# Second group's partial outputs through ScalarE and an adding DMA, lead copies on ScalarE, and passes taken group by group

## The chip, the cores and the metric

The program runs on one core of a Trainium2 chip. The metric is device time in microseconds (us) for one execution. Names of engines are those of the profile: PE (TensorE), with PEld for its weight loads, DVE (VectorE), ACT (ScalarE), POOL (GpSimd) and SP (SyncE, which here only issues DMAs). DMAs can be issued from SP, ACT and POOL; each of these works through its own list of instructions in order, and an instruction that waits holds everything behind it on the same engine.

## The reference

Local attention with a few global tokens, then a two-layer network with an ELU between the layers (sizes: batch 8, 8 heads, 512 local and 32 global tokens, head width 64; network 512 to 2048 to 512).

```python
def _attn_ref(q_l, k_l, v_l, q_g, k_g, v_g):
    ...
    s_g = scale * np.matmul(q_g, k_all.transpose(0, 1, 3, 2))
    out_g = np.matmul(sm(s_g), v_all)
    s_ll = scale * np.matmul(q_l, k_l.transpose(0, 1, 3, 2))
    mask = np.abs(pos[:, None] - pos[None, :]) <= window        # window = 32
    s_ll = np.where(mask, s_ll, -1000000000.0)
    s_lg = scale * np.matmul(q_l, k_g.transpose(0, 1, 3, 2))
    a_l = sm(np.concatenate([s_lg, s_ll], axis=-1))
    out_l = np.matmul(a_l, np.concatenate([v_g, v_l], axis=2))
    return np.concatenate([out_g, out_l], axis=2)

def _moe_ref(x, w_in, w_out):
    h = x @ w_in
    g = np.where(h > 0.0, h, np.exp(np.minimum(h, 0.0)) - 1.0)
    return g @ w_out
```

The attention output of all 4352 tokens is the input x of the network. The weights w_in and w_out come as 64-bit floats.

## The kernel before, in words

**Two streams.** A stream of attention stages and a stream of network work are interleaved into one program by a table of paces (`PACE`), and a scheduler then fixes the order of the instructions on each engine from its own estimates of when things become ready. At run time each engine simply follows that order. The tokens are cut into 17 blocks of 256: `blk` 0 to 15 local, 16 the global ones.

**The lead.** Until the first block's attention is done (`lead[0]`), only attention and the conversion of weights run. In `stage_t` the probabilities are transposed on PE into two PSUM banks, and two copies bring them to the tile `pt` in SBUF. In the lead, and again once all weights are there (`"f" in tab`), the first bank is copied by DVE and the second by ACT; in between both are copied by ACT. The copies are line 776. `stage_v` (L802, L809) multiplies `pt` with the values, L816 normalises the result into `tok`, L839 transposes it.

**Weights.** Sixteen units (`load_weights`, `unit`), alternating w_in and w_out, turn the raw 64-bit weights into two half-precision parts. A unit's raw tile (1 MB, two buffers) is loaded by SP (L164); ACT takes the absolute value (L178), POOL clamps it (L179), DVE does the integer work (L183, L187, L190, L194), ACT and DVE write the two parts (L211, L214). The raw tile of a w_in unit is free after L194, that of a w_out unit after ACT's L199. Tiles are numbered by creation: cu_146 belongs to the first unit, cu_1235 to the fifth, and the last two to w_in and w_out of the eighth pair (cu_2395 and cu_2491 before). When the last unit of a group has been converted, a small table (`tables`, L230 to L237) is made from the units' scales; it needs one transpose on PE (L131). The last tables are those named wm_c and wm_f.

**Blocks in passes.** The network's hidden width is cut into eight pairs p. While weights are still arriving, a block is done in three passes over groups of pairs, `"a"` (pairs 0 and 1), `"b"` (2 and 3), `"c"` (4 to 7). `ffn1` is the first layer (L315, 24 matmuls a pair) with the activation behind it (ACT L324 to L326 and L340, DVE L333 and L336); `ffn2`, two pairs later, is the second layer (L438, 12 matmuls a pair) into two PSUM accumulators `acc`. At the end of a pass the accumulators are emptied to tiles `o` (three buffers). A pass of group a empties with ACT (L449) and stores to a DRAM tile `od` (L450). Passes b and c first load `od` back into `o` (L431, issued from SP when the pass's second layer starts) and empty with DVE (L446: accumulator times scale plus `o`); b stores to `od` again, c to the output. Four blocks, 0 to 3, go through such passes. The others (group `"f"`) are done in one pass with a scheme of seven products on sums of the weights (`ffn2_seven`, L473), which needs the last tables and, per pair, `add_up` (L273 to L286).

**Which pass is next.** `choose` goes through the blocks in order and takes the first whose next group has a table. `scales` (L586 to L590 on POOL) computes the pass's scale factors `xs`; the activation on ACT waits for them. The order of passes that results is a0 a1 a2 b0 b1 b2 a3 c0 c1 c2 b3 c3.

Of the kernel before, what the change touches and what calls it, by code (L numbers as in the profile page):

```python
# [14 lines left out]
ALU = mybir.AluOpType  # L15
# [42 lines left out]
def attn_ffn(ctx: ExitStack, tc: tile.TileContext, qT, qgT, kT, vT, w_in, w_out, mask, out):  # L58
    nc = tc.nc
# [10 lines left out]
    od = {}  # L70

    def out_rows(blk, t):
        if blk < NBL:
            b, r = divmod(blk * BLK + t * P, SL)
            return out[b, SG + r:SG + r + P, :]
        return out[4 * t:4 * t + 4, 0:SG, :]
# [23 lines left out]
    lead = [True]  # L100
# [45 lines left out]
    tab = {}  # L146
# [150 lines left out]
    def ffn_stream():  # L297
# [119 lines left out]
        def ffn2():  # L417
            job, p, gh, gl = pend.pop(0)
            group, blk, _, _, sc, seven = job
            first, last = GROUPS[group][0], GROUPS[group][1] - 1  # L420
            if seven is not None:
                yield from ffn2_seven(blk, [(i, p, gh, gl) for i in range(len(SEVEN))], sc, seven)
                return
            if p == first:
                if group == "a":
                    od[blk] = dram.tile([2, P, DM], F32, name=f"od{blk}")
                state["acc"] = [ps_o.tile([P, DM], F32, name="acc") for _ in range(2)]
                state["o"] = [ffn.tile([P, DM], F32, name="o", bufs=3) for _ in range(2)]
                if group in "bc":
                    for t in range(2):  # L430
                        nc.sync.dma_start(state["o"][t], od[blk][t])  # L431
            acc = state["acc"]
            for t in range(2):
                for j in range(2):
                    s = slice(j * BLK + t * P, j * BLK + (t + 1) * P)
                    f = 2 * p + j
                    for k, (gt, wt) in enumerate(((gh, wout[0]), (gh, wout[1]), (gl, wout[0]))):
                        nc.tensor.matmul(acc[t], gt[:, s], wt[:, f, :], start=p == first and j == 0 and k == 0,  # L438
                                         stop=p == last and j == 1 and k == 2)
                    if j == 0:  # L440
                        yield
                if p == last:
                    o = state["o"][t]
                    oc = sc[:, 2 * NP:2 * NP + 1]
                    if group in "bc":
                        nc.vector.scalar_tensor_tensor(out=o, in0=acc[t], scalar=oc, in1=o,  # L446
                                                       op0=ALU.mult, op1=ALU.add)
                    else:
                        nc.scalar.activation(o, acc[t], AF.Copy, scale=oc)  # L449
                    nc.sync.dma_start(od[blk][t] if group in "ab" else out_rows(blk, t), o)  # L450
                yield
            uses[p] -= 1

# [127 lines left out]
        def scales(group, mx):  # L581
            sc = ffn.tile([P, 3 * NP + 1], F32, name="xs", bufs=4)
            wm, t = tab[group]
            o = GROUPS[group]
            r = slice(*o)
            nc.gpsimd.tensor_scalar(sc[:, r], isc[:, r], mx[:, 2:3], 1.0, ALU.mult, ALU.mult)  # L586
            nc.gpsimd.tensor_scalar(sc[:, 2 * NP + 1 + o[0]:2 * NP + 1 + o[1]], isc[:, r], mx[:, 2:3], -1.0,
                                    ALU.mult, ALU.mult)
            nc.gpsimd.tensor_scalar(sc[:, NP + o[0]:NP + o[1]], t[:, r], mx[:, 4:5], 2.0 ** -14, ALU.mult, ALU.mult)
            nc.gpsimd.tensor_scalar(sc[:, 2 * NP:2 * NP + 1], wm, mx[:, 2:3], 2.0 ** -17, ALU.mult, ALU.mult)  # L590
            return sc

        order = [*range(NBL - 1), NBL, NBL - 1]
        xs = {}
        step = dict.fromkeys(order, 0)
# [12 lines left out]

        def choose():

            for blk in order:
                if blk in xs and xs[blk][3] and step[blk] < 3:
                    group = "f" if "f" in tab and not step[blk] else "abc"[step[blk]]
                    if group in tab:
                        step[blk] += 3 if group == "f" else 1
                        xh, xl, mx, _ = xs[blk]
                        seven = [] if group == "f" else None
                        if seven is None:
                            for p in range(*GROUPS[group]):
                                uses[p] += 1  # L620
                        return group, blk, xh, xl, scales(group, mx), seven
# [6 lines left out]
        while left <= NBL:  # L628
            load()
            job = job or choose()  # L630
            if job is None:
                yield True
                continue
            cur, job = job, None
            group, blk = cur[:2]
            lo, hi = GROUPS[group]
            for p in range(lo, hi):
                load()
                yield from ffn1(cur, p)
                if len(pend) > LAG2:  # L640
                    yield from ffn2()
                if p == hi - 1:
                    job = choose()
            if group in "cf":
                del xs[blk]
                left += 1
# [22 lines left out]
    def attention():  # L669
# [91 lines left out]
        def stage_t(st, g, ts):  # L761

            n = len(ts)
            pt = apool.tile([P, 2, 4, P], F32, name="pt", bufs=1)
            for i, t in enumerate(ts):
                st["pt", g, t] = pt[:, t % 2]
            tp = [ps_a.tile([P, 512], F32, name="pa") for _ in range(2)]
            for i, t in enumerate(ts):
                for h in range(4):
                    for r in range(2):  # L770
                        rows = slice(64 * r, 64 * r + 64)
                        at = 64 * (4 * i + h)
                        nc.tensor.transpose(tp[r][:, at:at + 64], st["p", g, t][rows, h, :], ident[rows, rows])  # L773
            copies = (nc.vector.tensor_copy, nc.scalar.copy) if "f" in tab or lead[0] else (nc.scalar.copy,) * 2
            for r, copy in enumerate(copies):
                copy(pt[:, ts[0] % 2:ts[0] % 2 + n, :, 64 * r:64 * r + 64],
                     tp[r][:, 0:256 * n].rearrange("p (s h x) -> p s h x", s=n, h=4))
# [118 lines left out]
        for g in range(2):  # L896
            j = 4 * (1 + NT) * g
            if g:
                at(j - 8, "load", lambda: (load_queries(0, 1), load_heads(0, 1, "k")))
                at(j - 4, "load", lambda: load_heads(0, 1, "q"))  # L900
            at(j + 1, "S", lambda g=g: stage_sg(sts[0], g))
            at(j + 8, "T", lambda g=g: stage_tg(sts[0], g))
            for t in range(NT):
                i = j + 4 * (t + 1)
                at(i + 1, "S", lambda g=g, t=t: stage_s(sts[0], g, (t,)))
                at(i + 4, "load", lambda g=g, t=t: load_values(0, g, t))
                if t % 2:
                    at(i + 8, "T", lambda g=g, t=t: stage_t(sts[0], g, (t - 1, t)))
                    at(i + 11, "V", lambda g=g, t=t: stage_v(sts[0], g, t // 2))
                    at(i + 14, "X", lambda g=g, t=t: stage_x(sts[0], g, t // 2))  # L910
        for b in range(1, B):
# [9 lines left out]
            for n, (half, g) in enumerate((h, g) for h in range(2) for g in range(2)):  # L921
                i = base + 10 * n
                t = 2 * half
# [12 lines left out]
    f = ffn_stream()  # L936
# [90 lines left out]
```

## Time and profile before

| What | Value |
|---|---|
| median of 3 runs | 904.24 us (902.68 to 905.14) |
| the profiled execution | 900.32 us, of which span 898.3 us |
| PE busy | 852.4 us, 95% of the span |
| DVE busy | 677.0 us, 75% |
| ACT busy | 598.8 us, 67% |
| POOL busy | 77.7 us, 9% |
| chain that ended last | PE 56%, DVE 24%, ACT 13%, DMA 2% |
| loads of `od` from SP (L431) | 16, 256 KB each, 2.8 us from issue to landing |
| stores to `od` from SP (L450) | 16, 256 KB each, 2.6 us |

The span is the time from the first to the last instruction; about 2 us of the execution lie around it. All durations below come from that one execution. A row of a timeline gives the start, the duration, the engine and the line, and in square brackets the idle time of the engine before it with what ended it. A duration overlaps the start of the next instruction a little, so what an instruction costs its engine is the distance between two starts. "By stage" rows give the length of a stretch of time and then, engine by engine, the busy time and the count of instructions in it.

### The profile page before, as it was taken

The page shows a single profiled execution, that of the slowest core. Times are in us where ns is not written, and L with a number is a line of the kernel's source. Part 1 is how long each engine was busy: PE and PEld are TensorE (multiplying, and loading weights), DVE is VectorE, ACT ScalarE, POOL GpSimd, SP SyncE. Part 2 cuts the span into 40 slices and gives each one's busy share as a digit, 9 for nine tenths or more (in the row PEclk, how much of TensorE's full clock was granted, in tenths as well). Part 3 has the DMA queues.
Part 4 walks back from the last instruction along what each step waited for, and adds up shares of the span by engine and source line. Part 5 has one row for each costly group of instructions (what it writes and reads, how often), then busy time and mean ns, then how long its engine had stood idle before and what let it go on. Part 6 is the DMA issues. An engine that isn't in the chain of part 4 may idle for free.

```text
span 898.3 us, 27413 instructions
## 1 busy us (share of the span) xinstructions
PE 852.4 (95%) x11647; PEld 689.2 (77%) x11647; DVE 677.0 (75%) x1897; ACT 598.8 (67%) x1092; POOL 77.7 (9%) x124
## 2 busy tenths in 40 slices
PE   6678899899999999999999999999999999999997
PEld 3456566566766788888888887888878888888886
DVE  5997999997659867686767777776867677766566
ACT  4767888677557766666767675676667666666564
POOL 1111153230000100000000000000000000020000
PEclk8899999999999999999999999999999999999999
DMA  7985666424531435141530435133332211020000
GB/s 262 360 274 172 214 203 241 137 65 159 141 126 50 96 112 160 50 98 60 146 116 6 94 112 161 50 97 103 100 119 66 45 62 47 26 25 24 1 25 24
DMA packets 62513, 99.48 MB, mean 111 GB/s; under 512 B 31032, under 2 KB 31672, under 8 KB 62392
## 3 DMA queue, kind: packets, MB, share of 16 engines
q1 hardware_dynamic: 62104, 97.47, 34.8%
q8 instruction: 92, 1.51, 0.7%
q10 hardware_dynamic: 288, 0.26, 0.1%
q14 instruction: 29, 0.24, 0.1%
HBM read 78.32 MB, written 13.11 MB: 102 GB/s over the span
## 4 chain that ended last, share of the span: by engine, by line
PE 56%; DVE 24%; ACT 13%; DMA 2%; issue 2%; POOL 1%; SPq 0%; DVEq 0%; ACTq 0%; POOLq 0%
PE pa L315 22%; PE acc L473 11%; PE h L473 8%; PE h L315 4%; PE acc L438 4%; DVE gl L336 3%; ACT gh L352 2%; ACT p L756 2%; DVE gx L333 2%; ACT g L324 2%; DMA raw<-w_in 2%; PE pa L740 2%; PE pa L802 2%; PE pa L773 2%; DVE cu L190 2%
## 5 line engine op out<-in xcount | busy, mean ns | idle before, releaser
L315 PE MATMUL pa<-x,winh 128*128 128x256 f16 x1648 | 277.2, 273 | 2.3 <-ACT pg L710 1.7
L315 PEld LDWEIGHTS <-winh 128*128 128x128 f16 x2160 | 208.1, 98 | 41.1 <-issue 10.5
L315 PE MATMUL pa<-x,winl 128*128 128x256 f16 x824 | 224.6, 273 | 0.0
L352 ACT ACTIVATE gh<-gx,xs 128x896 f16<-128x896 f32 x103 | 107.5, 1044 | 142.1 <-DVE gx L349 142.1
L336 DVE SCALAR_TENSOR_TENSOR gl<-gx,xs,gh 128x896 f16<-128x896 f32 x103 | 118.4, 1150 | 74.4 <-ACT gh L352 74.3
L473 PEld LDWEIGHTS <-gh 128*128 128x128 f16 x1456 | 139.4, 98 | 20.3 <-issue 2.7
L333 DVE SCALAR_TENSOR_TENSOR gx<-g,hs 128x512 f32<-128x512 f32 x103 | 71.2, 691 | 77.8 <-ACT g L326 76.5
L315 PEld LDWEIGHTS <-winl 128*128 128x128 f16 x1080 | 105.7, 98 | 12.8 <-issue 0.2
L756 ACT ACTIVATE p<-p,m 128x128 f32<-128x128 f32 x256 | 81.4, 391 | 29.0 <-DVE m L751 29.0
L315 PE MATMUL h<-x,winh 128*128 128x256 f16 x512 | 86.6, 273 | 4.6 <-ACT hs L325 4.6
L473 PE MATMUL acc<-wouth,gh 128*128 128x256 f16 x312 | 85.2, 273 | 0.9 <-DVE o L446 0.9
L473 PE MATMUL acc<-wouth,gl 128*128 128x256 f16 x312 | 85.1, 273 | 0.0
L473 PE MATMUL acc<-woutl,gh 128*128 128x256 f16 x312 | 85.0, 273 | 0.0
L326 ACT ACTIVATE g<-g 128x512 f32<-128x512 f32 x135 | 84.9, 629 | 0.0
L324 ACT ACTIVATE g<-pa,xs 128x512 f32<-128x512 f32 x103 | 69.9, 678 | 20.8 <-PE pa L315 20.2
L473 PEld LDWEIGHTS <-gl 128*128 128x128 f16 x728 | 71.2, 98 | 9.3 <-DVE gl L336 1.0
L473 PE MATMUL h<-raw,gh 128*128 128x256 f16 x416 | 74.6, 273 | 0.0
L325 ACT ACTIVATE hs<-pa,xs 128x512 f32<-128x512 f32 x103 | 70.0, 679 | 0.0
L315 PE MATMUL h<-x,winl 128*128 128x256 f16 x256 | 69.8, 273 | 0.0
L586 POOL TENSOR_SCALAR xs<-isc,xm 128x8 f32<-128x8 f32 (+2 forms) x24 | 13.5, 563 | 569.3 <-DVE xm L115 396.7
L473 PE MATMUL h<-raw,gl 128*128 128x256 f16 x208 | 56.7, 273 | 0.0
L751 DVE CUSTOM_DVE_ANT_0 p<-pa,msk 128x128 f32<-128x128 f32 x224 | 50.1, 285 | 3.0 <-PE pa L740 3.0
(208 smaller groups left out, 1518.6 us busy)
## 6 DMA issues: line engine op xcount, KB each, us to landing
v<-vT SPq DMA_DIRECT2D x64, 520.0 KB, 4.7
k<-kT SPq DMA_DIRECT2D x32, 432.0 KB, 4.8
q<-qT SPq DMA_DIRECT2D x32, 256.0 KB, 5.4
raw<-w_in SPq DMA_DIRECT2D x8, 1024.0 KB, 5.4
raw<-w_out SPq DMA_DIRECT2D x8, 1024.0 KB, 5.6
out<-o SPq DMA_DIRECT2D x32, 256.0 KB, 2.8
od<-o SPq DMA_DIRECT2D x16, 256.0 KB, 2.6
o<-od SPq DMA_DIRECT2D x16, 256.0 KB, 2.8
```

What stands on the lines that cost most here:

```text
L190: nc.vector.scalar_tensor_tensor(out=ui, in0=high, scalar=-0x40000000, in1=ui, op0=ALU.bitwise_and, op1=ALU.bitwise_or)
L315: nc.tensor.matmul(h[:, j, :], wt[:, c, f], xt[:, c, :], start=k == 0, stop=k == 11)
L324: nc.scalar.activation(g, hf, AF.Relu, scale=sc[:, p:p + 1])
L325: nc.scalar.activation(hs, hf, AF.Copy, scale=sc[:, 2 * NP + 1 + p:2 * NP + 2 + p])
L326: nc.scalar.activation(g, g, AF.Exp, scale=-1.0)
L333: nc.vector.scalar_tensor_tensor(out=out, in0=ins[0], scalar=-1.0, in1=ins[1], op0=ALU.add, op1=ALU.max)
L336: nc.vector.scalar_tensor_tensor(out=dst, in0=src, scalar=sg, in1=hi, op0=ALU.mult, op1=ALU.subtract)
L352: nc.scalar.activation(gh, gx, AF.Copy, scale=sg)
L438: nc.tensor.matmul(acc[t], gt[:, s], wt[:, f, :], start=p == first and j == 0 and k == 0, stop=p == last and j == 1 and k == 2)
L473: nc.tensor.matmul(cols, gt, w, start=p == 0 and k == 0, stop=last and k == len(todo) - 1, skip_group_check=True)
L751: nc.vector.tensor_tensor_reduce(out=p[:, i, :], in0=sp[r][:, j * P:(j + 1) * P], in1=msk[:, mi, :], op0=ALU.add, op1=ALU.min, scale=-scal ...
L756: nc.scalar.activation(p[:, i, :], p[:, i, :], AF.Exp, bias=m[:, i:i + 1], scale=-1.0)
```

## The change

Three edits.

1. A pass of group b no longer loads `od`. Its accumulators are emptied by ACT, like those of group a, and POOL issues a DMA that adds the tile `o` to `od` in DRAM. Passes of group c are as before.
2. `choose` sorts the blocks: as long as the last tables are missing, a block with fewer passes behind it comes first; afterwards blocks not yet begun come after those that wait for their second pass, level with those that wait for their third.
3. In the lead both copies of `pt` are done by ACT.

```diff
@@ -426,7 +426,7 @@
                 state["o"] = [ffn.tile([P, DM], F32, name="o", bufs=3) for _ in range(2)]
-                if group in "bc":
+                if group == "c":
                     for t in range(2):
                         nc.sync.dma_start(state["o"][t], od[blk][t])
@@ -442,12 +442,15 @@
                 if p == last:
                     o = state["o"][t]
                     oc = sc[:, 2 * NP:2 * NP + 1]
-                    if group in "bc":
+                    if group == "c":
                         nc.vector.scalar_tensor_tensor(out=o, in0=acc[t], scalar=oc, in1=o,
                                                        op0=ALU.mult, op1=ALU.add)
                     else:
                         nc.scalar.activation(o, acc[t], AF.Copy, scale=oc)
-                    nc.sync.dma_start(od[blk][t] if group in "ab" else out_rows(blk, t), o)
+                    if group == "b":
+                        nc.gpsimd.dma_start(od[blk][t], o, accum_op=ALU.add)
+                    else:
+                        nc.sync.dma_start(od[blk][t] if group == "a" else out_rows(blk, t), o)
                 yield
@@ -608,7 +611,7 @@
         def choose():
-            for blk in order:
+            for blk in sorted(order, key=lambda b: step[b] if "f" not in tab or step[b] else 2):
                 if blk in xs and xs[blk][3] and step[blk] < 3:
@@ -771,7 +774,7 @@
-            copies = (nc.vector.tensor_copy, nc.scalar.copy) if "f" in tab or lead[0] else (nc.scalar.copy,) * 2
+            copies = (nc.vector.tensor_copy, nc.scalar.copy) if "f" in tab else (nc.scalar.copy,) * 2
```

In numbers: six of the 29 copies L776 on DVE go to ACT (35 there become 41); eight of the 16 adds L446 on DVE become eight more ACT copies L449; eight loads and eight stores leave SP's list, and eight DMAs enter POOL's. The order of passes becomes a0 a1 a2 b0 b1 a3 b2 b3 c0 c1 c2 c3. No matmul is added or removed. Behind line 446 the changed file's lines are numbered three higher. The scheduler's order changes at many places; three matter here.

On POOL, in the stretch where the last weight units are clamped, before (xs are scale factors, cu the units; the last two are cu_2395 and cu_2491):

```order
L179 TENSOR_SCALAR cu_2285<-cu_2285 128x1024
L586 TENSOR_SCALAR xs_2595<-isc_112,xm_1474 128x2
L587 TENSOR_SCALAR xs_2595<-isc_112,xm_1474 128x2
L590 TENSOR_SCALAR xs_2595<-wm_a_790,xm_1474 128x1
L589 TENSOR_SCALAR xs_2595<-t_a_791,xm_1474 128x2
L179 TENSOR_SCALAR cu_2395<-cu_2395 128x1024
L179 TENSOR_SCALAR cu_2491<-cu_2491 128x1024
```

and in the change (the last two units are cu_2393 and cu_2489; od0 and od1 are the DRAM tiles of blocks 0 and 1):

```order
L592 TENSOR_SCALAR xs_2452<-t_a_791,xm_1474 128x2
L451 DMA od0_1553<-o_2362 128x512
L451 DMA od0_1553<-o_2363 128x512
L592 TENSOR_SCALAR xs_2729<-t_b_1778,xm_1474 128x2
L593 TENSOR_SCALAR xs_2729<-wm_b_1777,xm_1474 128x1
L179 TENSOR_SCALAR cu_2393<-cu_2393 128x1024
L179 TENSOR_SCALAR cu_2489<-cu_2489 128x1024
L451 DMA od1_1801<-o_2495 128x512
```

The last two units now stand behind the two adding DMAs of block 0, which wait for ACT to empty that block's accumulators.

On PE, at the transposes of the last tables, before:

```order
L438 MATMUL acc_2755<-wouth_87,gl_2631 128x512
L438 LDWEIGHTS gh_2695
L438 MATMUL acc_2754<-wouth_87,gh_2695 128x512
L131 MATMUL pa_2632<-ident_76,wm_c_2582 128x128
L131 MATMUL pa_2647<-ident_76,wm_f_2591 128x128
```

and in the change:

```order
L315 MATMUL h_2738<-x16_2189,winl_86 128x256
L315 LDWEIGHTS winh_85
L315 MATMUL h_2738<-x16_2189,winh_85 128x256
L131 MATMUL pa_2628<-ident_76,wm_c_2578 128x128
L131 MATMUL pa_2642<-ident_76,wm_f_2587 128x128
```

These transposes stood behind 386 first-layer and 157 second-layer matmuls of the network, in the middle of block 3's first pass; they now stand behind 358 and 144, in block 3's second pass. The attention work ahead of them is the same.

On DVE, in the lead, around the second block's input x16_998 (cu_1235 is the fifth weight unit, pt_1156 a tile of turned probabilities), before:

```order
L567 SCALAR_TENSOR_TENSOR x16_998<-xr_489,xm_490,x16_998 128x1024
L776 COPY pt_1156<-pa_1157 128x8x64
L751 ISA p_1280,m_1279<-acc_1240,msk_75 128x128
L751 ISA m_1279 128x1
L194 SCALAR_TENSOR_TENSOR cu_1235<-raw_596,cu_1235 128x1024
L813 TENSOR_SCALAR sm_1181<-h_1180 128x4
```

and in the change, where the same L194 stands some sixty rows further ahead, before the first block's input is split:

```order
L132 TENSOR_REDUCE xm_346<-pa_956 128x1
L817 RECIPROCAL sm_893<-sm_893 128x8
L114 TENSOR_SCALAR xm_346<-xm_346 128x1
L194 SCALAR_TENSOR_TENSOR cu_1235<-raw_596,cu_1235 128x1024
L819 TENSOR_TENSOR tok_894<-h_891,sm_893 128x256
```

The copy is gone from DVE, and L194, which frees the raw tile for the next w_in load, comes earlier.

## The prediction

> **What bounds the kernel now.** I read the page's first rows, then busy time by stage, then the waits of PE one by one, then the chain of waits.
>
> ```profile
> span 898.3 us, 27413 instructions
> PE 852.4 (95%) x11647; PEld 689.2 (77%) x11647; DVE 677.0 (75%) x1897; ACT 598.8 (67%) x1092; POOL 77.7 (9%) x124
> ```
>
> ```profile
> 0.00:14.65 14.65, 9.43 (x128) 4.38 (x128) 3.76 (x27) 6.25 (x15) 2.50 (x8) 1.00 0.88 316
> 14.65:75.55 60.90, 42.58 (x1079) 30.18 (x1079) 56.81 (x208) 40.65 (x90) 9.26 (x13) 0.86 0.78 273
> 75.55:111.50 35.95, 31.69 (x393) 22.39 (x391) 31.06 (x81) 30.35 (x54) 4.13 (x7) 1.00 0.57 199
> 111.50:181.00 69.50, 63.36 (x645) 42.61 (x646) 65.88 (x146) 54.45 (x86) 26.74 (x29) 0.98 0.57 194
> 181.00:200.00 19.00, 19.00 (x186) 12.74 (x187) 17.44 (x46) 13.14 (x26) 7.50 (x10) 1.00 0.23 71
> 200.00:880.00 680.00, 674.38 (x9116) 566.62 (x9115) 490.60 (x1366) 446.77 (x810) 27.60 (x57) 1.00 0.29 82
> 880.00:898.30 18.30, 12.00 (x109) 10.28 (x106) 11.43 (x28) 7.15 (x15) 0.00 (x0) 0.96 0.09 30
> ```
>
> The columns are PE, PEld, DVE, ACT, POOL, the granted clock, the DMA share and GB/s. I cut at the first network matmul (75.55), at the transpose of group b's table (111.5) and at that of the last tables (181). From 181 to 880 PE is idle for 5.6 us in 699: this part is PE work and can't be had by these edits. Up to 181 the fullest engine is DVE: 56.81 of 60.90 in the lead, 65.88 of 69.50 in the last stretch. There PE waits, and its five long waits after the lead are these:
>
> ```profile
> 99.94 0.32 PE L131 MATMUL pa<-ident,cm 128*128 128x128 f32 x1 [2.24 <-ACT xr L840]
> 111.50 0.29 PE L131 MATMUL pa<-ident,wm_b 128*128 128x128 f32 x1 [2.02 <-DVE isc L237]
> 153.51 0.38 PE L315 MATMUL h<-x,winh 128*128 128x256 f16 x2 [1.87 <-ACT hs L325]
> 165.16 0.38 PE L315 MATMUL h<-x,winh 128*128 128x256 f16 x2 [0.86 <-ACT hs L325]
> 177.60 0.38 PE L315 MATMUL h<-x,winh 128*128 128x256 f16 x2 [1.86 <-ACT hs L325]
> ```
>
> 8.85 us in all. That is the most that can be won between 75 and 181, beside a shorter lead. The chain of waits says the same for the end of the stretch; its columns are start, length and what:
>
> ```profile
> 72.30 5.36 DMA raw<-w_in
> ...
> 157.27 6.46 DMA o<-od
> ...
> 183.73 2.40 PE h L315 x22
> ...
> 186.13 2.59 PE acc L438 x12
> ```
>
> After 181 it is matmuls, at 2.40/22 = 0.109 us for one of the first layer and 2.59/12 = 0.216 for one of the second. So the rule of the sum is: **the end moves by the change in the moment at which the last tables are ready, plus the PE work that the new order puts behind them.**
>
> **The change part by part.** DVE first. The groups:
>
> ```profile
> L776 ACT COPY pt<-pa 128x512 f32<-128x512 f32 x35 | 20.3, 582 | 4.6 <-PE pa L773 4.5
> L776 DVE COPY pt<-pa 128x512 f32<-128x512 f32 x29 | 19.8, 684 | 1.4 <-PE pa L773 1.4
> L446 DVE SCALAR_TENSOR_TENSOR o<-acc,xs,o 128x512 f32<-128x512 f32 x16 | 11.8, 743 | 4.5 <-PE acc L438 4.5
> L449 ACT ACTIVATE o<-acc,xs 128x512 f32<-128x512 f32 x8 | 5.4, 690 | 0.1
> ```
>
> and what one costs DVE from start to start:
>
> ```profile
> 40.37 0.68 DVE L776 COPY pt<-pa 128x512 f32<-128x512 f32 x1
> 40.97 0.68 DVE L187 TENSOR_SCALAR cu<-cu 128x1024 int32<-128x1024 int32 x1
> ...
> 155.60 0.74 DVE L446 SCALAR_TENSOR_TENSOR o<-acc,xs,o 128x512 f32<-128x512 f32 x1
> 156.26 0.14 DVE L120 TENSOR_SCALAR cm<-cm 128x1 int32<-128x1 int32 x1
> ```
>
> A copy is 0.60 us, an add 0.66. Six copies leave the lead: 3.6 us. Of the eight adds that go, the six of blocks 0 to 2 stand before the last tables: 4.0 us; block 3's two come after them, where PE is full and DVE is not the bound, and count for nothing. Against this the new order puts more of the first `add_up` ahead of the tables:
>
> ```profile
> 181.98 0.67 DVE L277 TENSOR_TENSOR tmp<-cu 128x512 f32<-128x512 f32 x1
> ...
> 186.88 0.42 DVE L278 TENSOR_TENSOR tmp<-cu 128x256 f32<-128x256 f32 x1
> 187.22 0.68 DVE L286 TENSOR_TENSOR raw<-tmp,raw 128x512 f16<-128x512 f32 x1
> ```
>
> 1.5 us from start to start. DVE's work up to the tables falls by 3.6 + 4.0 - 1.5 = 6.1 us.
>
> Then two waits go. The first L324 stands behind an L178 that waits for a raw load, and late in the stretch ACT waits for the scale factors of block 0's third pass:
>
> ```profile
> 77.68 1.14 ACT L178 ACTIVATE cu<-raw 128x1024 f32<-128x1024 f32 x1 [1.34 <-DMA raw<-w_in]
> 78.72 0.68 ACT L324 ACTIVATE g<-h,xs 128x512 f32<-128x512 f32 x1
> ...
> 175.67 0.69 ACT L324 ACTIVATE g<-h,xs 128x512 f32<-128x512 f32 x1 [4.46 <-POOL xs L586]
> ...
> 177.00 0.75 DVE L336 SCALAR_TENSOR_TENSOR gl<-g,xs,gh 128x512 f16<-128x512 f32 x1 [0.84 <-ACT gh L340]
> ```
>
> The load at 72.30 waits for the L194 that now stands sixty rows further ahead, so the 1.34 go; the queue on SP in front of that load becomes the next to be late. At 175 the new order has passes b2 and b3 to run, whose factors need no late table. Of ACT's 4.46 us only what DVE loses counts: 0.84 here, and with the two short waits after it I take 1.5.
>
> ACT gets six copies (0.58 each, 3.5 us in a stretch where it has 20 us free) and eight L449 (0.69 each, 5.5 us beside 15 free). Two copies in series instead of side by side make a `pt` 0.6 us later: six times that, 3.5 us, if each is awaited, nothing where DVE's queue was longer. I take nothing, since in the lead DVE is the fuller engine.
>
> POOL is where a cost is unknown, as the trace has no DMA issued there. Two adding DMAs of block 0 stand in front of the last two L179, and what waits for those is L183 on DVE, which holds all of DVE. POOL's rows:
>
> ```profile
> 58.06 0.26 POOL L590 TENSOR_SCALAR xs<-wm_a,xm 128x1 f32<-128x1 f32 x1
> ...
> 112.67 1.33 POOL L587 TENSOR_SCALAR xs<-isc,xm 128x2 f32<-128x2 f32 x1
> ...
> 138.50 1.04 POOL L179 TENSOR_SCALAR cu<-cu 128x1024 f32<-128x1024 f32 x1 [5.22 <-ACT cu L178]
> ...
> 163.14 3.22 POOL L179 TENSOR_SCALAR cu<-cu 128x1024 f32<-128x1024 f32 x1 [6.57 <-ACT cu L178]
> ```
>
> The same operation takes 0.26 or 1.33, and 1.04 or 3.22, the long ones while DVE is full. So an issue is bounded by 0.26 and 3.22. I take 1.3, the middle of the small operations' long times. The second tile `o` is written by ACT about 1 us before the unit's L178 ends, so of 2 x 1.3 some 1.6 are hidden, and the unit is 1.0 late. Bounds: 0 and 6.4.
>
> The transfers themselves:
>
> ```profile
> od<-o SPq DMA_DIRECT2D x16, 256.0 KB, 2.6
> o<-od SPq DMA_DIRECT2D x16, 256.0 KB, 2.8
> ```
>
> An adding transfer reads and writes DRAM: between 2.6 and 2.6 + 2.8 = 5.4 us. Its reader is the load for group c, four passes later, and its buffer is wanted again three tiles, over 10 us of PE work, later. Both hide it; without that cover ACT would wait up to 5.4 once. The loads and stores that leave SP count for nothing: during the 6.46 us of the chain's `o<-od`, DVE had other work.
>
> The sum: tables earlier by 6.1 + 1.3 + 1.5 - 1.0 = 7.9 us. PE work put behind them: 386 - 358 = 28 first-layer matmuls (3.1 us) and 157 - 144 = 13 of the second (2.8), 5.9 together. So the end comes 2.0 us earlier: the profiled execution from 900.32 to 898.3, its span to 896.3, and the median from 904.24 to **902.2**. (The profiled execution lies 3.9 below the median; I move both by the same.)
>
> **The rivals.** *PE never waits for the tables.* If the weights chain gets ahead by more than I count, PE's waits at 111.5, 153.5, 165.2 and 177.6 close: 2.02 + 1.87 + 0.86 + 1.86 = 6.6 us, 897.6. For it: three of the four end in ACT `hs`, which was late through DVE and POOL. Against it: PE now reaches every table with less work behind it, so the same wait may only move there.
>
> *POOL's issues are slow.* If an issue beside a full DVE takes the 3.22 us of the L179 at 163.14, the last w_in unit and with it DVE's L183 come 6.4 late instead of 1.0: 902.2 + 5.4 = 907.6, slower than before. It decides from the point where the two issues cost over 3 us. For it: the long rows above, and DVE's 65.88 of 69.50. Against it: most POOL rows there are near 1.2. [...]
>
> *The lead isn't shorter.* If loads (0.78 of the DMA engines in the lead) or the two copies in series hold it, the 3.6 are not won: 902.2 + 3.6 = 905.8.
>
> **How the numbers follow.** My forecast 0.42, with its own range 900 to 904.5; PE free of table waits 0.28; slow issues 0.16; lead not shorter 0.14. The range that leaves out at most 2 in 10 is 897 to 908. About 0.3%, 2.7 us, is what a measurement of this kernel can tell from no change: below 901.5 is faster, above 906.9 slower. Faster: the second case and a third of the first, 0.41. Slower: most of the third and a little of the fourth, 0.17. Same: 0.42.
>
> **What would show it.** On PE's timeline the transposes of the last tables at about 173, with a wait of 1 to 4 us before them; first network matmul near 72; DVE's copies down to 23 and its adds to 8; ACT's wait at 175 gone; the last two L179 not more than 2 us behind their L178. It is wrong if the first matmul isn't earlier, if DVE waits more than 3 us for POOL, or if PE idles after 181.

## The result: slower by 1.0%

The changed kernel takes 913.31 us (median, 911.53 to 914.73), the kernel before on the same chip 903.66: ratio 1.0101, 95% interval 1.0087 to 1.0116. The forecast was 902.2, with a range up to 908. The page's first rows of the profile after:

```profile
span 910.9 us, 27409 instructions
PE 861.9 (95%) x11647; PEld 694.8 (76%) x11647; DVE 668.6 (73%) x1883; ACT 607.3 (67%) x1106; POOL 95.1 (10%) x132
```

The span is 12.6 longer than in the profile before (898.3). PE ran the same 11647 matmuls, yet was busy 861.9 us instead of 852.4, so its matmuls took 9.5 us longer in all and its waits are 3.1 longer. The granted clock is lower in the same places, but slower matmuls lengthen the kernel only where something waits for them, so this is no split of the 12.6. Busy time by stage, cut where the prediction cut:

```profile
14.65:75.55 60.90, 44.99 (x1069) 32.46 (x1069) 51.25 (x198) 44.03 (x97) 7.22 (x13) 0.76 0.77 283
75.55:111.50 35.95, 32.73 (x376) 22.49 (x377) 27.60 (x73) 26.43 (x48) 4.17 (x7) 0.88 0.50 174
111.50:181.00 69.50, 57.23 (x583) 37.53 (x581) 60.25 (x137) 52.23 (x84) 30.75 (x29) 0.95 0.57 166
181.00:200.00 19.00, 18.45 (x130) 12.51 (x129) 18.98 (x40) 15.61 (x27) 10.83 (x13) 1.00 0.18 43
```

The clock is 0.76, 0.88 and 0.95 where it was 0.86, 1.00 and 0.98; from 181 to the end, taken as one stretch, it is 1.00 in both. DVE did lose work (51.25 in the lead against 56.81, 60.25 in the third stretch against 65.88), and PE did less all the same: 583 matmuls against 645. The last tables, on PE's timeline:

```profile
188.17 0.32 PE L131 MATMUL pa<-ident,wm_c 128*128 128x128 f32 x1 [0.55 <-DVE wm_c L231]
```

188.2 instead of 180.9 and of the 173 that was forecast. With the 5.9 us of PE work put behind them, 7.3 + 5.9 = 13.2, and the span grew by 12.6: the rule of the sum held, the tables went the wrong way. The chain of waits of the profile after shows where, in order of time:

```profile
137.12 1.15 DVE cu L194
138.29 6.34 DMA raw<-w_in
...
146.94 4.91 DMA raw<-w_out
151.88 1.15 ACT cu L178
153.09 1.42 POOL cu L179
154.59 1.10 POOL xs L589
...
163.06 1.96 POOL od L451 x2
165.79 1.05 POOL cu L179
166.86 1.22 DVE cm L183
```

Between 153.09 and 166.86 the chain is nothing but POOL: a clamp, the scale factors of two passes, the two adding DMAs, two more scale factors, and the clamp of the last w_in unit.

### The profile page after: what moved, and what is told of

It reads as the page before. It is cut to its first block, busy times and chain, and to the rows that moved or that the text cites. A ratio compares the mean times of both kernels' runs of the same rounds, so it can differ in the third digit from the quotient of the medians.

```text
span 910.9 us, 27409 instructions
## 1 busy us (share of the span) xinstructions
PE 861.9 (95%) x11647; PEld 694.8 (76%) x11647; DVE 668.6 (73%) x1883; ACT 607.3 (67%) x1106; POOL 95.1 (10%) x132
## 4 chain that ended last, share of the span: by engine, by line
PE 64%; DVE 17%; ACT 13%; DMA 3%; issue 2%; POOL 2%; SPq 0%; DVEq 0%; ACTq 0%
PE pa L315 24%; PE acc L476 11%; PE h L476 8%; PE h L315 5%; PE acc L438 5%; ACT p L759 3%; DVE gl L336 3%; PE pa L805 2%; PE pa L743 2%; PE pa L776 2%; ACT gh L352 2%; DMA raw<-w_in 2%; ACT g L324 1%; DVE gx L333 1%; ACT hs L325 1%
## 5 line engine op out<-in xcount | busy, mean ns | idle before, releaser
L336 DVE SCALAR_TENSOR_TENSOR gl<-gx,xs,gh 128x896 f16<-128x896 f32 x103 | 118.5, 1151 | 74.7 <-ACT gh L352 74.5
L315 PE MATMUL h<-x,winh 128*128 128x256 f16 x512 | 91.8, 282 | 1.4 <-ACT x L567 1.3
L324 ACT ACTIVATE g<-pa,xs 128x512 f32<-128x512 f32 x103 | 70.2, 681 | 21.5 <-PE pa L315 21.1
L589 POOL TENSOR_SCALAR xs<-isc,xm 128x8 f32<-128x8 f32 (+2 forms) x24 | 24.8, 1033 | 551.4 <-DVE xm L115 390.6
L315 PE MATMUL h<-x,winl 128*128 128x256 f16 x256 | 72.3, 282 | 0.0
```

Source lines behind the costliest of these rows:

```text
L315: nc.tensor.matmul(h[:, j, :], wt[:, c, f], xt[:, c, :], start=k == 0, stop=k == 11)
L324: nc.scalar.activation(g, hf, AF.Relu, scale=sc[:, p:p + 1])
L336: nc.vector.scalar_tensor_tensor(out=dst, in0=src, scalar=sg, in1=hi, op0=ALU.mult, op1=ALU.subtract)
```

## The experiments

Ratios are to the kernel before, run on the same chip each time; "clock" is the mean granted clock of a kernel's executions (0.980 for the kernel before, over 97 of them); "tables" is when PE transposes the last tables in the profiled execution.

| Run | Ratio (95%) | Clock | First network matmul, tables (us) |
|---|---|---|---|
| the change | 1.0101 (1.0087 to 1.0116) | 0.973 | 77.9, 188.2 |
| e1 copies only | 1.0033 (1.0019 to 1.0047) | 0.978 | 77.8, 187.4 |
| e2 order of passes only | 1.0036 (1.0018 to 1.0054) | 0.978 | 76.8, 181.7 |
| e3 group b only | 1.0038 (1.0023 to 1.0053) | 0.979 | 78.0, 186.1 |
| e4 change without copies | 1.0068 (1.0053 to 1.0083) | 0.977 | 76.7, 184.2 |
| e5 before, PE kept busy in the lead | 0.9972 (0.9953 to 0.9991) | 0.990 | 74.5, 180.9 |
| e6 change, PE kept busy | 1.0049 (1.0033 to 1.0065) | 0.984 | 81.2, 188.9 |
| e7 change, no DMA on POOL | 1.0059 (1.0040 to 1.0078) | 0.976 | 77.4, 185.0 |
| e8 before, a second profile | 901.65 us, once | 0.986 | 76.8, 182.3 |
| e9 copies only, PE kept busy | 0.9983 (0.9970 to 0.9997) | 0.988 | 76.6, 184.9 |
| e10 group b by a second DRAM tile | 1.0043 (1.0028 to 1.0058) | 0.977 | 76.7, 183.4 |
| e11 the same, PE kept busy | 0.9997 (0.9982 to 1.0012) | 0.986 | 77.4, 180.9 |
| e12 all edits, both causes out | 1.0029 (1.0015 to 1.0043) | 0.984 | 77.9, 181.9 |
| e13 before, adds of group b twice | 1.0034 (1.0020 to 1.0048) | 0.979 | 75.3, 183.6 |
| e14 before, third raw tile | 1.0058 (1.0041 to 1.0075) | 0.979 | 80.8, 187.3 |
| e15 control of e14 | 1.0051 (1.0032 to 1.0069) | 0.980 | 77.0, 184.9 |

The last column is of one execution each. Those of e3 and e6 are the longest of their runs (908.88 and 912.87, medians 906.83 and 908.73), those of e13 and e15 the shortest (903.71 and 904.16, medians 906.38 and 908.53).

### e1 to e4: one edit at a time

e1 is the third edit alone, as its lines stand in the diff of the change.

> Only the third edit: both pt copies on ScalarE in the lead. Theory (lead): in the changed kernel the first network matmul came at 77.9 us instead of 75.5, at half clock for 3 us more, since the two copies stand in series, PE waits for them, and its clock falls; this edit alone then gives a first matmul near 78, units 3 us later, and about 907 (+3.3). Rival (order and POOL): the lead is late only because the scheduler's order of everything changed with the other two edits; then this edit alone gives a first matmul near 73 to 75.5 and 901 to 904.

e2 is the second alone.

> Only the second edit: passes sorted by step. 26 first-layer and 9 second-layer matmuls, 4.8 us of PE work, stand behind the last tables instead of ahead of them. Theory (work put behind): the tables come no more than 1.5 us earlier, so the end is 3 to 5 us later, about 907. Rival (the tables follow): with less PE work ahead the tables come 4 to 5 us earlier and the time stays at 903.7, within 1.5.

e3 is the first alone.

> Only the first edit: group b through ScalarE and the adding DMA. 12 first-layer and 1 second-layer matmuls (1.5 us) stand behind the tables. Theory (POOL in the way): the last w_in unit's L183 waits 2 to 4 us for POOL, which eats what DVE saves (4.0); tables 0 to 1 us earlier, 904 to 905. Rival (DVE decides): tables 3 to 4 us earlier, first matmul unchanged at 75.5, 901 to 902.

e4 is the first and second together.

> The change without the third edit (copies as before). Theory (lead): the 3.3 us of the lead come back: 910, first matmul at 75.5. Rival (order and POOL): time as the change, 912 to 914, with a first matmul near 78 too.

Each edit alone is slower by about 0.35%, and within the errors they add: 0.33 + 0.36 + 0.38 = 1.07, where the three together measure 1.01; the first and second make 0.74, where e4 measures 0.68. So there is no one culprit, and no part that paid. For e1 and e2 the first of the two theories was met. For e3 neither was: it is slower than both, with L183 waiting only 1.7 us. e4 came out lower than either theory's 910 and 912.

In e2 PE hardly waits at the tables:

```profile
181.67 0.32 PE L131 MATMUL pa<-ident,wm_c 128*128 128x128 f32 x1 [0.78 <-DVE wm_c L231]
```

They come 0.6 earlier than in the second profile of the kernel before (182.3, e8), and 4.8 us of PE work stand behind them that stood ahead. That is 4.2 by the rule; the spans, 903.5 and 899.6, differ by 3.9.

### e5, e6, e8: the clock in the lead

e5 and e6 give PE something to do where it waits. The added transposes write a tile that the next instruction overwrites:

```diff
                 tp = ps_a.tile([P, 512], F32, name="pa")
+                for _ in range(8 if lead[0] else 0):
+                    nc.tensor.transpose(tp[:, 0:P], ident, ident)
                 for j in range(2):
...
                 tp = ps_a.tile([P, 512], F32, name="pa")
+                for _ in range(6 if lead[0] and half == 0 else 0):
+                    nc.tensor.transpose(tp[:, 0:P], ident, ident)
                 for i in range(3):
```

> The kernel before with 72 idle-time transposes of the identity on PE in the lead (8 ahead of each L839 group, 6 ahead of each first L721), written to the tile that is overwritten next; nothing else. They fill PE's waits, some 20 us of them. Theory (clock): PE's granted clock in the lead, 0.86 in the profile before, goes to 0.95 or more, the first network matmul comes 1 to 3 us earlier and the time falls to about 901. Rival (DVE sets the lead, the clock follows): the clock rises, the time stays within 1 us of 903.2 or grows by the transposes that are in the way.

> The changed kernel with the same 72 transposes in the lead. Theory (clock): half of the change's loss in the lead is half clock (PE at 0.5 from 67 to 80.5 us): the clock in the lead goes from 0.76 to 0.95 or more, the first network matmul from 77.9 to about 75, the time from 913 to about 909. Rival (two copies in series and order): the clock rises and the first matmul stays at 77 to 78, the time at 912 to 914.

> The kernel before, unchanged, for a second profile: the first, 900.3, was the fastest of its runs and had the highest clock. If the clock of the lead is a matter of chance from run to run, a run near 903 shows a clock of 0.76 to 0.82 in the lead and a first network matmul 1 to 2 us later than 75.5; if it belongs to the kernel, it shows 0.86 and 75.5 again and is late elsewhere.

They are 64 (40 and 24), not the 72 of the expectations. The lead of e5, from 14.65 to its first network matmul:

```profile
14.65:74.45 59.80, 47.16 (x1136) 34.04 (x1137) 56.43 (x210) 40.70 (x90) 8.81 (x13) 0.92 0.82 292
```

The clock is 0.92 (the expectation had 0.95 or more), and e5 is 0.28% faster than the kernel before; it adds instructions and removes none. Of the versions here only e5 and, by less, e9 beat both kernels. The change gains by the same filling too: 1.0101 becomes 1.0049, about the time that the theory named. But the kernel before gains 0.28% by it, so what the change loses goes from 1.01% to 0.77%, and the 0.24 between them is within the summed error of about 0.3. That filling pays is shown; how much of the change's own loss is half clock isn't. The profile of e6 doesn't help: its first network matmul is at 81.2, later than in the change.

e8 tells how to read the profile of before. Over the 97 executions of that kernel the clock went from 0.970 to 0.988 and the time from 900.36 to 906.30, with a correlation of -0.71 and 2.6 us for 0.01 of clock. The profile on which the prediction rests (900.32 at 0.988) is the short end of that spread; e8 (901.65 at 0.986) is near it. Single profiles of this kernel differ by such amounts, so the verdicts here go by the ratios. e8 was not near the 903 that its expectation asked for, so it decides little; its clock in the lead was 0.83, its first matmul came 1.3 us later than in the first profile, and its span is 1.3 longer.

### e7 and e10: POOL

e7 is the changed kernel with a plain store from SP in place of the adding DMA, so that it leaves out the sum with group a's part:

```diff
-                        nc.gpsimd.dma_start(od[blk][t], o, accum_op=ALU.add)
+                        nc.sync.dma_start(od[blk][t], o)
```

> The changed kernel with group b's tile o stored by a plain DMA from SP instead of the adding DMA from POOL. The sum with group a's part is left out; all of ScalarE's copies stay, and the order of passes. Theory (POOL in the way): the 3.9 us that L183 waits for POOL near 167 fall under 1, the last tables come 3 us earlier, and the time falls to about 910. Rival (POOL's queue is late by its own scale factors, or DVE would be the bound anyway): L183 still waits 2 us or the tables come no earlier; 912 to 914.

The change goes from 1.0101 to 1.0059, some 3.8 us. POOL's timeline of the changed kernel, and then of e7 (start, duration, line):

```profile
160.58 1.72 POOL L592 TENSOR_SCALAR xs<-t_b,xm 128x2 f32<-128x2 f32 x1
...
162.73 0.27 POOL L592 TENSOR_SCALAR xs<-t_a,xm 128x2 f32<-128x2 f32 x1
163.06 1.96 POOL L451 DMA_DIRECT2D od<-o  x2
165.11 0.26 POOL L592 TENSOR_SCALAR xs<-t_b,xm 128x2 f32<-128x2 f32 x1
165.44 0.27 POOL L593 TENSOR_SCALAR xs<-wm_b,xm 128x1 f32<-128x1 f32 x1
165.79 1.04 POOL L179 TENSOR_SCALAR cu<-cu 128x1024 f32<-128x1024 f32 x1
```

```profile
154.25 1.10 POOL L589 TENSOR_SCALAR xs<-isc,xm 128x2 f32<-128x2 f32 x1
...
162.24 0.27 POOL L593 TENSOR_SCALAR xs<-wm_b,xm 128x1 f32<-128x1 f32 x1
162.59 1.04 POOL L179 TENSOR_SCALAR cu<-cu 128x1024 f32<-128x1024 f32 x1
```

The two issues cost 2.05 us from start to start. Ahead of them stands the larger part, 8 us of small operations for two passes, and it stays in e7. So L183 waits 3.86 in the change, and 2.20 in e7; the tables come 3.2 earlier. Time and tables are as the theory had them, the wait that is left is the rival's. In this queue the slow operations are those beside a full DVE: the six from 154.59 to 160.58 take 0.71 to 1.74, in 8 us (154 to 162) in which DVE was busy for all 8.00, L592 among them with 1.72 at 160.58; at 165.11, while DVE waits for POOL, L592 takes 0.26. A full DVE isn't enough, though: L592 takes 0.27 at 162.73, where DVE was still busy (0.27 of 0.27). The group of all eight issues, with their busy time, the mean in ns, and POOL's idle time before them:

```profile
L451 POOL DMA_DIRECT2D od<-o x8 | 7.3, 992 | 8.8 <-ACT o L449 4.8 <-ACT p L759 3.1 <-ACT cu L282 0.8
```

e10 takes the DMAs off POOL in the first edit alone, with the computation complete:

```diff
-                    od[blk] = dram.tile([2, P, DM], F32, name=f"od{blk}")
+                    od[blk] = dram.tile([4, P, DM], F32, name=f"od{blk}")
...
+                        nc.gpsimd.dma_start(state["o"][t], od[blk][2 + t], accum_op=ALU.add)
...
+                    nc.sync.dma_start(od[blk][t] if group == "a" else od[blk][2 + t] if group == "b" else out_rows(blk, t), o)
```

> Only the first edit, but with nothing on POOL while weights arrive: group b is emptied by ScalarE and stored by SP to a second DRAM tile; a pass of group c, which comes after the last tables, loads the first part and adds the second with a DMA from POOL. Theory (POOL in the way): the first edit's loss (ratio 1.0038) is the adding DMAs ahead of the last two L179; without them L183 near 160 waits under 1.5 us and the time is 902 to 903.5. Rival (ScalarE's copies and the order are the loss): 905 to 907 as before.

1.0043: no better than e3, and as the rival had it. L183 no longer waits there (1.70 in e3), but the time is the same within the error. The theory fell: alone, the first edit shows no cost of POOL, while the change does (e7). What differs is that the second edit puts two passes' scale factors in a row ahead of the last units. Where e10 loses time is seen on PE:

```profile
179.31 0.38 PE L315 MATMUL h<-x,winh 128*128 128x256 f16 x2
...
183.39 0.47 PE L131 MATMUL pa<-ident,wm_c 128*128 128x128 f32 x1 [3.37 <-DVE wm_c L231]
...
184.08 0.64 PE L315 MATMUL h<-x,winh 128*128 128x256 f16 x2
```

The stretch right behind it, with busy time by engine and the clock as in the tables of stages:

```profile
182.70:189.30 6.60, 5.91 (x20) 3.14 (x21) 5.67 (x18) 4.41 (x8) 3.86 (x6) 0.50 0.01 2
```

PE, with 12 first-layer matmuls less ahead, waits 3.4 us at the tables; after that its clock is 0.50 for 6.6 us, 5.9 of them busy, and a pair of matmuls is shown at 0.64 instead of 0.38. e3 waits there as long (3.36), in its longest execution. That these two things are the first edit's whole loss isn't shown.

### e9, e11, e12: the causes taken out

e9 is e1, and e11 is e10, each with the filling transposes of e5 (the diffs above together).

> The third edit alone (both copies on ScalarE in the lead) with the 72 filling transposes, to set beside the kernel before with the same transposes (900.5, ratio 0.997). Theory (clock): what the third edit costs (ratio 1.0033) is half clock in the lead; with PE kept busy it costs nothing: 900 to 901.5, first matmul at 74 to 75. Rival (two copies in series hold the lead): the cost stays, 903 to 904.5, with DVE still waiting some 4 us for PE's value products.

> The same with the 72 filling transposes in the lead: the version that could beat both. If the two gains add: 899 to 901, faster than before by 0.3 to 0.5%. If the filling transposes only gain what the order loses (here 360 and 156 network matmuls stand ahead of the last tables, before 386 and 157): 901 to 904.

e9 (902.5) lies between its two theories. Against e5 it is 0.9983 to 0.9972: of the copies' 0.33%, 0.11 is left, each with an error of about 0.2, so the two runs don't tell whether the cost went. By the profiles the two copies in series still show in the lead: in e9 DVE waits 3.1 us for PE's value products, in e5 it has no such wait, and the first matmul is at 76.6 against 74.5; but e9's profile (904.17) is of one of its longer executions. e11 is no faster than the kernel before, and 0.25 behind e5, as its second theory had it.

e12 has all three edits, the second DRAM tile of e10 and the filling of e5:

> All three edits, with the two causes taken out together: group b by way of the second DRAM tile (no DMA on POOL before the last tables) and the 72 filling transposes in the lead. The order of passes stays, so 28 first-layer and 13 second-layer matmuls (5.9 us) still stand behind the last tables. If the causes add (change 1.0101, less 0.0042 for POOL, less 0.0052 for the clock of the lead): ratio 1.001, about 904, with L183's wait under 2.5 us and the tables near 182. If they are the same loss seen twice: 1.005 or more, 908. If nothing but these two was wrong and the prediction's sum holds otherwise: 0.995 to 0.998, 899 to 902.

1.0029, a little above what adding gives (1.001), within the summed error; L183's wait (2.21) and the tables (181.9) are as that theory had them. It is 0.57% (5.2 us) behind e5. By their profiles the tables are 1.1 later and 5.9 us of PE work stand behind them, 7.0 by the rule against 6.1 between the spans (904.3 and 898.2). So with the DMAs off POOL and the lead filled, the second edit's work behind the tables is nearly all that is left, and the tables still come no earlier, with less for DVE to do.

### e13 to e15: what sets the pace of the units

e13 adds work to DVE in the kernel before:

```diff
+                    if group == "b":
+                        spare = ffn.tile([P, DM], F32, name="tmp", bufs=3)
+                        nc.vector.scalar_tensor_tensor(out=spare, in0=acc[t], scalar=oc, in1=o,
+                                                       op0=ALU.mult, op1=ALU.add)
```

> The kernel before with group b's eight adds on DVE done twice (the first time into a spare tile): six more adds, 4.0 us of DVE, ahead of the last tables; 9 first-layer matmuls more (1.0 us) stand ahead of the tables than before. Theory (the units' loop sets the pace): tables and time as before, 903 to 904.5, DVE's idle time smaller. Rival (DVE's amount of work sets it, as the prediction's sum had it): tables 4 us later, 906.5 to 907.5.

e14 gives the raw loads a third tile, and takes one from `xr` and one from `v` to make room; e15 only takes those two.

```diff
-        raw = ffn.tile([P, NC, 2 * P, 2] if m == 0 else [P, 2, DM, 2], I32, name="raw")
+        raw = ffn.tile([P, NC, 2 * P, 2] if m == 0 else [P, 2, DM, 2], I32, name="raw", bufs=3)
...
-        return ffn.tile([P, 2, DM], F32, name="xr", bufs=3), ffn.tile([P, 10], F32, name="xm", bufs=NX + 4)
+        return ffn.tile([P, 2, DM], F32, name="xr", bufs=2), ffn.tile([P, 10], F32, name="xm", bufs=NX + 4)
...
-            v = apool.tile([P, NQ, 4, DV], F32, name="v", bufs=3)
+            v = apool.tile([P, NQ, 4, DV], F32, name="v", bufs=2)
```

> The kernel before with three raw tiles instead of two, for which xr has two buffers instead of three and v two instead of three. Theory (loop): raw loads no longer wait for the unit before last, from the fourth pair's L183 to the last L194 it takes 4 to 8 us less than 88, the tables come that much earlier and the time falls 2 to 4 us under the control. Rival (DVE): the loads come earlier, the stretch still takes 87 to 89, time as the control.

> The control: xr and v with two buffers, raw with two as before. Fewer buffers can only make the lead and the attention later: 903 to 908, stretch of the units 88 to 90.

The stretch to compare runs from the fourth pair's L183 to the last L194. Busy time in it, of the kernel before, the change, e10, e12 and e13 in this order (columns as before, so the third is DVE):

```profile
86.10:174.30 88.20, 79.80 (x836) 53.36 (x834) 85.35 (x201) 71.91 (x118) 27.27 (x30) 0.98 0.61 209
```

```profile
89.20:183.60 94.40, 79.65 (x797) 51.30 (x795) 83.26 (x199) 74.04 (x123) 33.89 (x35) 0.95 0.59 179
```

```profile
88.60:176.60 88.00, 80.23 (x829) 52.59 (x827) 84.41 (x198) 75.39 (x125) 29.27 (x30) 0.98 0.57 194
```

```profile
88.00:177.30 89.30, 77.61 (x795) 50.52 (x794) 83.24 (x197) 73.62 (x123) 28.59 (x31) 0.96 0.56 189
```

```profile
87.00:178.80 91.80, 82.06 (x841) 54.09 (x840) 88.30 (x204) 72.59 (x120) 28.28 (x31) 0.96 0.58 196
```

Adding and taking away aren't alike. With 3 us more on DVE (e13) the stretch is 3.6 longer (e8, the same kernel as before, has 88.3), and the kernel 0.34% slower: the theory of a loop with slack fell. With 1 or 2 us less (e10, e12) it is no shorter, 88.0 and 89.3, and DVE waits more. A third raw tile brings no time, 1.0058 against the control's 1.0051, yet it doesn't settle the loads' part: its stretch is 1.3 shorter than the control's (89.9 against 91.2, itself above the 88 to 90 expected), but its lead is 3.7 longer. The account that fits is that DVE's work and the units' way through loads, ScalarE and POOL are about equally long, so that shortening the one shows the other. It is argued, not shown: what e10 and e12 take off DVE they put on ScalarE (71.91 us busy in the stretch before, 75.39 and 73.62 there), and no run here takes DVE's work away without that. Which single wait takes over in e12 isn't settled.

## Why the prediction was wrong

**What bounds the kernel, and the rule** (the end moves with the tables and with the PE work behind them): right. It gives the spans within 1.2 us in the change, e1, e2, e4, e7 and e12; in e3 and e10 it falls 2 to 3 us short, and there PE waited at the tables and went on at half clock; in e13 it falls 1.5 short, for which no cause is shown. What failed is the moment of the tables: 7.9 us earlier by the sum, 7.3 later in the profile. The terms of that moment follow.

**PE work put behind, 5.9 us**: right in size, and the main thing that stays when the rest is mended (e12).

**The lead, -3.6 us for six copies**: the first step that failed. It took each copy off DVE as time off the lead, and put the later `pt` of two copies in series at nothing, "since in the lead DVE is the fuller engine". DVE's busy time in the lead fell by 5.6, and the first matmul came 2.4 later. What DVE did with the gap, before and after, by its waits in the lead (microseconds in total, times, longest):

```profile
DVE sm L813 <- PE h L802: 0.7, 1, 0.7
```

```profile
DVE sm L816 <- PE h L805: 4.7, 2, 2.6
```

It waited for PE's products, and PE ran from 67 to 80.5 at half clock, where the kernel before had 0.87. The first row is of the change, the second of e3, which leaves DVE its copies:

```profile
67.00:80.50 13.50, 10.42 (x131) 7.78 (x131) 6.38 (x30) 8.94 (x22) 2.04 (x5) 0.50 0.60 219
67.00:80.50 13.50, 10.29 (x136) 7.59 (x135) 8.57 (x36) 8.98 (x22) 1.01 (x4) 0.54 0.58 214
```

Half clock by itself doesn't make DVE wait so: with 0.54 in e3 and 0.62 in e2 it waited 1.8 and 1.5 us in all for PE's value products, in the change 5.4 and in e1 5.7 (before 1.2). So that wait comes with the third edit, whose two copies stand in series, as the rival "the lead isn't shorter" had it. Half clock costs time as well (the first 24 matmuls of the network, right behind the lead, take 3.89 us on the chain of waits, where at 0.109 each they would take 2.6). It was in no part of the prediction, though the row that it quoted showed 0.86; but it isn't the copies' doing alone, since e2 and e3 have 0.76 and 0.77 in the lead without them, e1 and the change 0.76. How the 2.4 us divide between the two is open.

**DVE's middle, -4.0 + 1.5**: the work was counted well (85.35 to 83.26 in the stretch of the units), the conclusion failed. DVE's idle time there rose from 2.9 to 11.1 us. In the stretch from 86 to 175 before, and from 89 to 184 after, DVE waited for POOL's clamp:

```profile
DVE cu L187 <- POOL cu L179: 1.3, 1, 1.3
```

```profile
DVE cm L183 <- POOL cu L179: 6.2, 3, 3.9
DVE cu L187 <- POOL cu L179: 1.6, 1, 1.6
```

"Tables earlier by DVE's sum" needs DVE to be the only long way. In e10 and e12 it had less work in the stretch and the stretch was no shorter, so it isn't.

**POOL, +1.0**: the price of an issue was taken as 1.3 and measured 0.99. The two issues ahead of the last units don't test the rival of 3.22, since DVE was waiting meanwhile; the next two ran beside a DVE that was busy all the time, and took no longer (DVE is the third column):

```profile
163.06:165.02 1.96, 1.96 (x10) 0.88 (x9) 0.00 (x0) 1.89 (x3) 1.96 (x2) 1.00 0.44 17
176.57:178.39 1.82, 1.82 (x14) 1.15 (x13) 1.82 (x4) 0.93 (x2) 1.82 (x3) 1.00 0.35 20
```

So that price fell for the DVE operations met here: none of the eight issues took over 1.24 us. (The rival's 6.4 us also left out the 1.6 that the prediction's own term takes as hidden.) Yet the wait that the rival described came: L183 waited 3.86 us, by a queue of 8 us of scale factors ahead of the DMAs, which was not counted; the order shown for the change has only the last of them. Taking the DMAs away won 0.42%.

**The waits, -1.3 and -1.5**: the 1.34 ahead of the first L324 and ACT's 4.46 at 175 are gone, as forecast, but moved nothing: that L324 now waits 3.35 us for PE's first network matmuls, and at 175 the units were late already.

**The offset** (profile 3.9 under the median, the same for both): the offset went with the clock (0.988 in the profile of before and 0.980 on average, 0.975 and 0.973 for the change) and wasn't the same. The change's profile lies 0.6 under its median.

Of the rivals, PE free of table waits saw the waits that it names close (the 2.02 at group b's table became 0.56, the three behind `hs` are gone), and others come in their place: between the first network matmul and the last tables PE's waits add up to 15.2 us, before to 10.2.

## What to carry to other kernels

Work that leaves a busy engine need not bring time: look first at what else in the stage is nearly as long, and at the engine that takes the work over, since added work may cost in full what removed work doesn't bring (3 us more on DVE made the stretch 3.6 longer in e13, 1 or 2 less made it no shorter in e10 and e12). Where a DMA or a wait moves to a quiet engine's queue, add up everything that the new order puts in front of it there, not only its own price (here 8 us of scale factors ahead of two issues of 2.05). And where PE waits a lot at the start, read the granted clock as a cost of its own: filling the waits was worth more here (0.28%, e5) than any of the three edits, each of which alone was 0.33 to 0.38% slower.

## What was new about the hardware

Half clock followed one PE wait of 2.01 us, and didn't follow another of 2.20. Rows of the change's PE timeline, of which the first is followed by a clock of 0.50 from 67 to 80.5 and the second by 1.00 (136 to 140):

```profile
66.07 0.88 PE L724 MATMUL pa<-ident,pg 128*128 128x128 f32 x6 [2.01 <-ACT pg L714]
```

```profile
136.05 0.70 PE L776 MATMUL pa<-ident,p 64*128 64x64 f32 x8 [2.20 <-ACT xr L843]
```

The wait of 3.37 us in e10 is followed by half clock too (0.50 from 182.7 to 189.3). So the length of the wait just ahead doesn't by itself decide it in these three cases; what does isn't shown by any run here. The clock also varies from run to run in the same kernel: 0.970 to 0.988 in the kernel before. By the slope of 2.6 us for 0.01 that range goes with an estimated 4.7 us, more than the 2.0 that this change was expected to bring.

An adding DMA from POOL landed as late as a plain store in the change, by the medians, with the issue included:

```profile
od<-o SPq DMA_DIRECT2D x8, 256.0 KB, 4.2
od<-o POOLq DMA_DIRECT2D x8, 256.0 KB, 4.2
```

Both are later than the plain stores before (2.6). In e3 it was 4.6 against 3.9, and in e10, where the adding DMA goes from DRAM to SBUF, 5.7 against 2.7 for a plain load. One by one the eight of the change landed after 3.8 to 7.4 us, where the prediction's estimate was 2.6 to 5.4.
